# Two small matrix products per unit spread over all four 64x64 quadrants of TensorE, in a kernel that runs a linear-attention recurrence and a mixture of experts

## The chip, the cores and the metric

The kernel runs on one core of one Trainium2 chip. The metric is the device time of one execution in microseconds (us); lower is better. Before the change it was 1084.33 us, the median of 3 runs (1083.53 to 1084.63). The engines are called PE (TensorE matmul), PEld (TensorE's weight loads), ACT (ScalarE), DVE (VectorE), POOL (GpSimd) and SP (SyncE, which issues most transfers here).

## The reference

Two blocks follow each other. The first is a recurrence over 768 tokens, for 4 batches and 8 heads, with a 40x40 state per head; the second a mixture of 4 experts on the 3072 rows of 320 numbers that the first leaves.

```python
for t in range(S):
    y[:, :, t] = np.einsum('bhd,bhde->bhe', rt, state)
    Sa = np.einsum('bhde,bhe->bhd', state, at)
    state_decay = state * wt[:, :, None, :] - np.einsum('bhd,bhe->bhde', Sa, bt)
    state = state_decay + np.einsum('bhd,bhe->bhde', vt, kt)
...
p = domain_probs / (domain_probs.sum(-1, keepdims=True) + 1e-09)
for e in range(E):
    h = np.maximum(x @ w1[e], 0.0)
    out += p[:, e:e + 1] * (h @ w2[e])
```

All numbers are float32.

## The kernel before, in words

**Units.** The recurrence is cut into 12 chunks of 64 tokens. A unit is one chunk of two of the four batches: two batches x 64 tokens fill the 128 partitions, and the 8 heads lie beside each other. There are 24 units, numbered 0 to 23; units 0 and 1 are chunk 0, and so on. Within a chunk the recurrence becomes products of 64x64 matrices, among them the inverse of a triangular 64x64 matrix per batch and head.

**Stages of a unit.** `within` (L451) prepares a unit: decays (G, gp), the scaled inputs N, K and AT, their transposed copies NT and KT (ACT), and the score matrices. The scores pc are masked into VC by DVE (`causal`, L449, two copies, one per bank), pe into ET in the same way, and pfe becomes F (ACT, L580), the matrix to be inverted. `substitute` (L627) inverts the four 32x32 diagonal blocks of it: ACT and DVE copy them out (blocks, L632), DVE forms M, and POOL (DVE in unit 0) substitutes forward over 32 columns (tile Z, L670 and L687). `merge` (L693) makes the 64x64 inverse out of the 32x32 ones. `step` (L731) then runs the unit's step of the recurrence: prn (products with the state), psat, pxr, pdy, and the result Y, which goes to the mixture as xT. The mixture's products (ph, p, po) are cut into pieces and put between the recurrence's products, so that PE has dense work while others prepare the next small product.

**The order on the engines.** PE's instructions run in the order in which the code makes them (`stated`, `in_order`; `matmul` is the helper at L110, so every product has that line). DVE's order is written out in `VECTOR_ORDER` for a large part of the work. ACT's order is set by a scheduler from priorities (`sooner` raises one). In the main loop the order on PE around the change is, for units 6 to 22: the transposes pNT and pKT, the product pc of a later unit, then pY of `merge`, then prn of `step` (two products, with AT and with the identity), a first part of ph, pQ of `merge`, the rest of ph and a product p of the mixture.

**Quadrants.** Small products use 64 rows (contraction) by 64 columns (output partitions) of the 128x128 array: a quadrant is a row half and a column half. `quadrants` (L432) issues the heads of a product in the order of `QUADS`, which visits all four quadrants, and gives each row half its own PSUM bank (`banks`, two of them). `two_heads` inside `merge` (L709) is different: row half r always goes to column half r, into one bank.

**PSUM.** The eight banks are dealt from two pools: `big`, five banks, for the recurrence, and `mm`, three banks, for the mixture. A tile that asks for a bank of `big` gets one that an earlier tile has left, and its first matmul waits until the copy out of that earlier tile is done. The five banks go round among pg, pNT, pKT, pc (2), pY (1), prn (2), pQ (1), pfe (2), psat (2), pe (2), pxr (2), pev (2) and pdy (2).

**The merge.** Z's result is transposed into Qc and QTc (DVE). First product: pY, of below and QTc (below is the off-diagonal 32x32 block of F, copied by POOL), copied by ACT to Yq with four copies of 32 partitions x 128 elements. Second: pQ, of Qc and Yq, copied with four more into the off-diagonal block of QT (the diagonal blocks of QT are POOL's copies, L705). psat and the product after it read QT.

Of the kernel before, what the change touches and what calls it, by code (L numbers as in the profile page):

```python
# [33 lines left out]
def kernel(  # L34
# [38 lines left out]
    nc = tc.nc  # L73

    B, H, S, D = r.shape
# [3 lines left out]
    Q = 32  # L79
# [10 lines left out]
    def noted(ins, name, n=None, i=None):  # L90
        if n is None:
            n = sum(k.startswith(name) for k in made)
        key = f"{name}{n}" if i is None else f"{name}{n}.{i}"
        made[key] = ins
        if key in names:
            stated_order.append(ins)
        return ins

    def keep(ins):

        if not any(ins is x for x in stated_order):
            tc.keep_in_program_order(ins)
# [6 lines left out]
    def matmul(**k):  # L109
        return stated(nc.tensor.matmul(**k))  # L110
# [11 lines left out]
    def of_mixture(name):  # L122
# [6 lines left out]
        out=ident[:], in_=ident[:], pattern=[[1, P]], compare_op=ALU.is_equal, fill=0.0,  # L129
# [5 lines left out]
    for t, n, op in ((upf, L, ALU.is_gt), (diagf, Q, ALU.is_equal)):  # L135
        nc.vector.memset(t[:], 1.0)
        for q in range(P // n):
            o = slice(q * n, (q + 1) * n)
            nc.gpsimd.affine_select(
                out=t[o], in_=t[o], pattern=[[1, n]], compare_op=op, fill=0.0, base=0, channel_multiplier=-1,  # L140
# [3 lines left out]
    def dealt(x):  # L144

        return x.rearrange("p h (k g) -> p k g h", g=4)
# [54 lines left out]
    for n, a_sum in enumerate(("a1", "a7", "a5", "a2")):  # L201
        t = padded["RV"[n % 2], n // 2] = sb.tile([P, H, 64], FP32, name="padded", tag=a_sum)
# [21 lines left out]
    def sooner(wanted):  # L224
        return tc.high_priority(offset=SOONER) if wanted else nullcontext()
# [68 lines left out]
    ins = nc.vector.transpose(out=unit_cols[:], in_=dealt(diagf[:, None, :].to_broadcast([P, H, Q])))  # L294
# [88 lines left out]
    def half(s):  # L383
        return slice(64 * s, 64 * s + 64)

    def quarter(q):
        return slice(Q * q, Q * q + Q)

    def of_slot(x, s):

        return x.rearrange("p (j s) e -> p j s e", s=2)[:, :, s, :]
# [301 lines left out]
    def merge(q):  # L693


        Qc = sb.tile([P, H, Q], FP32, name="Qc", tag="q", bufs=2)
        QTc = sb.tile([P, H, Q], FP32, name="QTc", tag="q", bufs=2)
        keep(noted(nc.vector.transpose(out=dealt(Qc[:]), in_=q.Z), "Qc", q.u))
        ins = nc.vector.transpose(  # L699
            out=QTc[:].rearrange("p h r -> p (h r)"), in_=Qc[:].rearrange("p h c -> p (h c)"),  # L700
        )
        keep(noted(ins, "QTc", q.u))
        q.QT = QTs()
        for i in range(P // Q):
            ins = nc.gpsimd.tensor_copy(out=q.QT[quarter(i), :, quarter(i % 2)], in_=QTc[quarter(i)])  # L705
            tc.keep_in_program_order(ins)
        yield

        def two_heads(name, lhsT, rhs, to):  # L709
            p = (of_mixture if q.u == 0 and name == "pY" else big)(name)  # L710
            for n in range(NJ):
                for r in range(2):
                    matmul(
                        out=p[half(r), n * 2 * Q:(n + 1) * 2 * Q], lhsT=lhsT[half(r), 2 * n:2 * n + 2, :],
                        rhs=rhs[half(r), 2 * n:2 * n + 2, :], start=True, stop=True,
                    )
            for r in range(2):
                for y in range(2):
                    src = p[quarter(2 * r + y), 0:H * Q].rearrange("p (n two t) -> p n two t", two=2, t=Q)[:, :, y, :]
                    with sooner(name == "pY"):  # L720
                        ins = nc.scalar.copy(out=of_slot(to[quarter(2 * r)], y), in_=src)
                    noted(ins, name + "c", q.u, 2 * r + y)

        Y = Ys()
        two_heads("pY", q.below, QTc, Y)
        yield

        two_heads("pQ", Qc, Y, q.QT[:, :, quarter(1)])
        yield

# [476 lines left out]
    for u in range(1, NU):  # L1207
        in_order[0] = True
        q = units[u]
# [149 lines left out]
```

## Time and profile before

| | |
|---|---|
| median of 3 runs | 1084.33 us |
| span of the profiled execution, first to last instruction | 1081.0 us |
| what the runs have beyond that span | 3.3 us |
| mean granted TensorE clock | 0.995 |
| PE busy, 0 to 54 us | 44.80 of 54.00 us |
| PE busy, 54 to 234 us | 178.02 of 180.00 us |
| PE busy, 277 to 948 us | 671.00 of 671.00 us |
| ACT busy, 277 to 948 us | 227.90 us |
| DVE busy, 277 to 948 us | 488.22 us |
| matmul records of pY, of pQ | 384 and 384, 16 a unit |
| ACT copies Yq<-pY, QT<-pQ | 96 and 96, 4 a unit, 0.256 us each |

The profile is one execution; its time is given as the span, and the run's time has some us around it. Times within it are counted from the start of the span. A matmul of 32-bit numbers shows as two records of the profile, and a weight load as two as well. The view called timeline merges neighbouring instructions of one kind: start, length, engine, line, operation, output<-input, tile and shape, count, and in brackets how long the engine was idle before and what released it.

### The profile page before, as it was taken

The page shows a single profiled execution, that of the slowest core. Times are in us where ns is not written, and L with a number is a line of the kernel's source. Part 1 is how long each engine was busy: PE and PEld are TensorE (multiplying, and loading weights), DVE is VectorE, ACT ScalarE, POOL GpSimd, SP SyncE. Part 2 cuts the span into 40 slices and gives each one's busy share as a digit, 9 for nine tenths or more (in the row PEclk, how much of TensorE's full clock was granted, in tenths as well). Part 3 has the DMA queues.
Part 4 walks back from the last instruction along what each step waited for, and adds up shares of the span by engine and source line. Part 5 has one row for each costly group of instructions (what it writes and reads, how often), then busy time and mean ns, then how long its engine had stood idle before and what let it go on. Part 6 is the DMA issues. An engine that isn't in the chain of part 4 may idle for free.

```text
span 1081.0 us, 38617 instructions
## 1 busy us (share of the span) xinstructions
PE 1066.3 (99%) x16140; PEld 960.2 (89%) x16140; DVE 760.2 (70%) x1549; ACT 353.3 (33%) x958; POOL 494.2 (46%) x1276
## 2 busy tenths in 40 slices
PE   7899999999999999999999999999999999999998
PEld 7788888899999999999999999999989999998888
DVE  7687779897776866877777768668767776534343
ACT  3442435333333424224333334242333333221110
POOL 5116777765264373473562643734725626420000
PEclk9899999999999999999999999999999999999999
DMA  7877645435436445444364363454443532322320
GB/s 117 228 188 211 145 107 125 89 103 142 100 87 155 110 104 127 114 108 112 91 138 100 97 148 96 102 124 109 115 94 107 133 88 62 98 76 78 104 78 13
DMA packets 268870, 122.20 MB, mean 113 GB/s; under 512 B 213736, under 2 KB 242072, under 8 KB 268696
## 3 DMA queue, kind: packets, MB, share of 16 engines
q1 hardware_dynamic: 264712, 118.90, 45.1%
q8 instruction: 127, 2.08, 0.8%
q10 hardware_dynamic: 3984, 0.84, 0.4%
q14 instruction: 47, 0.39, 0.1%
HBM read 111.79 MB, written 3.93 MB: 107 GB/s over the span
## 4 chain that ended last, share of the span: by engine, by line
PE 86%; POOL 8%; DVE 3%; issue 2%; ACT 1%; DMA 0%; ACTq 0%; DVEq 0%; POOLq 0%
PE ph L110 36%; PE p L110 30%; POOL Z L687 5%; POOL Z L670 3%; PE pdy L110 3%; PE psat L110 2%; PE pxr L110 2%; PE prn L110 2%; PE po L110 2%; PE pc L110 1%; PE pfe L110 1%; PE pev L110 1%; PE pe L110 1%; PE warm L110 1%; PE pQ L110 1%
## 5 line engine op out<-in xcount | busy, mean ns | idle before, releaser
L110 PE MATMUL ph<-xT,w1p 128*128 128x256 f32 (+3 forms) x3040 | 441.6, 375 | 0.1
L110 PEld LDWEIGHTS ph<-xT,w1p 64*64 64x64 f32 (+1 forms) x3040 | 336.9, 161 | 53.8 <-issue 13.0
L687 POOL TENSOR_TENSOR Z<-Z 128x31 f32<-128x31 f32 (+7 forms) x704 | 261.3, 371 | 55.2
L1000 DVE TENSOR_TENSOR a<-hs 128x512 f32<-128x512 f32 x220 | 152.5, 711 | 107.8 <-ACT hs L877 107.8
L877 ACT ACTIVATE hs<-ph 128x512 f32<-128x512 f32 (+1 forms) x208 | 116.8, 564 | 322.6 <-PE ph L110 322.2
L670 POOL TENSOR_TENSOR Z<-M,Z 128x62 f32<-128x62 f32 (+7 forms) x352 | 145.7, 414 | 95.0 <-DVE M L656 69.2
L110 PE MATMUL p<-sums,a 128*128 128x160 f32 x1056 | 164.9, 299 | 0.0
L110 PEld LDWEIGHTS p<-sums,a 128*128 128x128 f32 x1056 | 152.8, 190 | 2.2
L892 DVE SCALAR_TENSOR_TENSOR osb<-p,gate,osb 128x320 f32<-128x320 f32 (+1 forms) x243 | 108.0, 481 | 65.6 <-PE p L110 60.3
L637 POOL COPY below<-F 32x256 f32<-32x256 f32 x48 | 21.3, 443 | 232.8 <-ACT F L580 231.1
L110 PEld LDWEIGHTS p<-w,hs 128*128 128x128 f32 x704 | 98.6, 190 | 8.5 <-issue 7.3
L110 PE MATMUL p<-w,hs 128*128 128x160 f32 x704 | 104.9, 302 | 0.0
L110 PE MATMUL p<-w,a 128*128 128x160 f32 x704 | 102.8, 299 | 0.0
L110 PEld LDWEIGHTS p<-w,a 128*128 128x128 f32 x704 | 98.0, 190 | 0.0
L705 POOL COPY QT<-QTc 32x256 f32<-32x256 f32 x96 | 40.3, 420 | 72.7 <-DVE QTc L699 67.2
L797 ACT COPY RS<-pxr 64x256 f32<-64x256 f32 x88 | 32.2, 366 | 102.7 <-DVE SX L449 79.6
L618 ACT COPY EV<-pev 64x160 f32<-64x160 f32 x96 | 23.0, 286 | 90.5 <-PE pev L110 90.1
L518 DVE RECIPROCAL gp<-gp 128x320 f32<-128x320 f32 x24 | 51.6, 2151 | 0.7
L640 DVE STREAM_TRANSPOSE M<-blocks 128x1024 f32<-128x1024 f32 x24 | 47.2, 1967 | 2.6 <-ACT blocks L632 2.5
L449 DVE COPY_PREDICATED VC<-mask_up,pc 128x256 f32<-128x256 int32 x48 | 18.7, 443 | 40.8 <-PE pc L110 40.8
L580 ACT COPY F<-pfe 128x256 f32<-128x256 f32 x48 | 15.6, 376 | 79.6 <-PE pfe L110 78.7
L110 PE MATMUL pdy<-VC,k_tok 64*64 64x104 f32 (+1 forms) x768 | 38.4, 259 | 2.6 <-issue 2.6
(151 smaller groups left out, 1346.7 us busy)
## 6 DMA issues: line engine op xcount, KB each, us to landing
w1p<-in_moe_w_dram SPq DMA_DIRECT2D x95, 512.0 KB
w1p<-in_moe_w_dram SPq DMA_DIRECT2D x190, 64.0 KB
w<-in_moe_w_dram SPq DMA_DIRECT2D x4, 1280.0 KB
sums<-in_moe_w_dram SPq DMA_DIRECT2D x9, 512.0 KB
natW<-in_w_dram SPq DMA_DIRECT2D x48, 80.0 KB
natB<-in_b_dram SPq DMA_DIRECT2D x48, 80.0 KB
natK<-in_k_dram SPq DMA_DIRECT2D x48, 80.0 KB
out_dram<-osb SPq DMA_DIRECT2D x45, 80.0 KB
```

Source lines behind the costliest of these rows:

```text
L110: return stated(nc.tensor.matmul(**k))
L518: pin(noted(nc.vector.reciprocal(out=gp[:], in_=gp[:]), "1/gp", q.u))
L618: nc.scalar.copy(out=of_slot(q.EV[half(p)], i ^ p)[:, :, 0:D], in_=pev[i][half(p)])
L637: tc.keep_in_program_order(nc.gpsimd.tensor_copy(out=q.below[quarter(i)], in_=q.F[quarter(i), :, 0:Q]))
L640: ins = nc.vector.transpose(out=M[:], in_=cols)
L670: ins = eng.tensor_tensor(out=Z[:, 1:3, 0:n, j + 1:Q], in0=M[:, j:j + 2, None, j + 1:Q].to_broadcast([P, 2, n, m]), in1=Z[:, here, 0:n, j: ...
L687: eng.tensor_tensor(out=z[:, 0], in0=z[:, 0], in1=z[:, x], op=ALU.add)
L705: ins = nc.gpsimd.tensor_copy(out=q.QT[quarter(i), :, quarter(i % 2)], in_=QTc[quarter(i)])
L797: nc.scalar.copy(out=RS[half(s), x ^ s::2], in_=prs[x][half(s)].rearrange("p (j i) t -> p j i t", i=2),)
L877: ins = nc.scalar.activation(out=h[:, i * HF // 2:(i + 1) * HF // 2, 0:n], in_=ph[i][:], func=ACTF.Relu,)
L892: ins = nc.vector.scalar_tensor_tensor(out=to, in0=p, scalar=sc, in1=to, op0=ALU.mult, op1=ALU.add)
L1000: ins = nc.vector.tensor_tensor(out=t[:], in0=x, in1=y, op=op)
```

## The change

`two_heads` takes two banks, one for each row half r of the operands. The n-th pair of heads writes the column half r for even n and the other one for odd n, so that the eight matmuls of a product visit the quadrants (0,0), (1,1), (0,1), (1,0) twice. The results of even and odd pairs now lie in different partition halves of a bank, so each copy out of PSUM is split in two by `odd`: eight copies of 32 partitions x 64 elements in place of four of 32 x 128. Both products of all 24 units are made so; in unit 0 the two banks of pY are from the pool `mm`.

```diff
         def two_heads(name, lhsT, rhs, to):
-            p = (of_mixture if q.u == 0 and name == "pY" else big)(name)
+            p = [(of_mixture if q.u == 0 and name == "pY" else big)(name) for _ in range(2)]
             for n in range(NJ):
                 for r in range(2):
                     matmul(
-                        out=p[half(r), n * 2 * Q:(n + 1) * 2 * Q], lhsT=lhsT[half(r), 2 * n:2 * n + 2, :],
+                        out=p[r][half(r ^ n % 2), n * 2 * Q:(n + 1) * 2 * Q], lhsT=lhsT[half(r), 2 * n:2 * n + 2, :],
                         rhs=rhs[half(r), 2 * n:2 * n + 2, :], start=True, stop=True,
                     )
             for r in range(2):
-                for y in range(2):
-                    src = p[quarter(2 * r + y), 0:H * Q].rearrange("p (n two t) -> p n two t", two=2, t=Q)[:, :, y, :]
-                    with sooner(name == "pY"):
-                        ins = nc.scalar.copy(out=of_slot(to[quarter(2 * r)], y), in_=src)
-                    noted(ins, name + "c", q.u, 2 * r + y)
+                for odd in range(2):
+                    for y in range(2):
+                        src = p[r][quarter(2 * (r ^ odd) + y), 0:H * Q]
+                        src = src.rearrange("p (n two t) -> p n two t", two=2, t=Q)[:, odd::2, y, :]
+                        with sooner(name == "pY"):
+                            ins = nc.scalar.copy(out=of_slot(to[quarter(2 * r)], y)[:, odd::2, :], in_=src)
+                        noted(ins, name + "c", q.u, 4 * r + 2 * odd + y)
```

## The prediction

> **What bounds the kernel now.** I read the page first, its busy rows and the slices.
>
> ```profile
> span 1081.0 us, 38617 instructions
> PE 1066.3 (99%) x16140; PEld 960.2 (89%) x16140; DVE 760.2 (70%) x1549; ACT 353.3 (33%) x958; POOL 494.2 (46%) x1276
> PEclk9899999999999999999999999999999999999999
> ```
>
> TensorE is busy for 1066.3 of 1081.0 us at a granted clock of 0.995. Cut into stretches, 277 to 948 us has PE busy for 671.00 of 671.00 us, so there every nanosecond added to or taken from PE's queue arrives at the end. Before 234 us the chain of waits runs for long pieces through POOL Z (the inverse of units 3 to 6); there PE idles about 1 us between 108 and 234 us, so two chains run nearly level.
>
> Next the timeline of one steady unit, PE alone. A matmul of this kernel is two records, so a two_heads product (8 matmuls) is 16, a four-quadrant product (16 matmuls) is 32.
>
> ```profile
> 574.24 0.69 PE L110 MATMUL pc<-RT,VT 40*64 40x64 f32 x32
> 574.75 0.57 PE L110 MATMUL pY<-QTc,below 64*64 64x64 f32 x13
> 575.18 0.59 PE L110 MATMUL prn<-state,AT 64*64 64x40 f32 x28
> 576.15 0.39 PE L110 MATMUL ph<-xT,w1p 64*64 64x256 f32 x2
> ...
> 577.02 0.63 PE L110 MATMUL pQ<-Yq,Qc 64*64 64x64 f32 x16
> 577.58 0.48 PE L110 MATMUL ph<-xT,w1p 128*128 128x256 f32 x1
> ...
> 595.56 0.65 PE L110 MATMUL pxr<-RT,SaT 64*64 64x64 f32 x32
> 596.03 0.65 PE L110 MATMUL pxr<-RT,SN 64*64 64x64 f32 x32
> ```
>
> The reader is to see the pace. pxr, which uses all four quadrants in the order the change gives to pY and pQ, moves 32 records in 596.03 - 595.56 = 0.47 us, 0.0147 us each. In the records pQ starts a pair (one per diagonal quadrant) every 0.058 us: 16 records take 8 x 0.058 = 0.47 us, half the work in the same time. Then the same unit on ACT and DVE.
>
> ```profile
> 574.43 0.60 ACT L524 COPY KT<-pKT 128x512 f32<-128x512 f32 x1
> 575.43 1.07 ACT L721 COPY Yq<-pY 32x128 f32<-32x128 f32 x4 [0.40 <-PE pY L110]
> 577.70 1.06 ACT L721 COPY QT<-pQ 32x128 f32<-32x128 f32 x4 [0.18 <-PE pQ L110]
> ...
> 575.00 0.79 DVE L449 COPY_PREDICATED VC<-mask_up,pc 128x256 f32<-128x256 int32 x2 [2.26 <-PE pc L110]
> ```
>
> The first VC copy empties pc's second bank; it takes 0.444 us (median of its 48), so it ends at 575.44. Today nobody near waits for it: prn has begun at 575.11.
>
> **The change part by part.** *PE, removed:* each product goes from 0.47 to 16 x 0.0147 = 0.235 us, a gain of 0.23 us. The trace has it for pxr, pe and prn, so I take it as it is; 48 products would give 11.3 us if nothing waited.
>
> The Trainium skill, TensorEngine Tiling (Array Packing), section Theoretical Speedup, promises up to 2x for each dimension of 64 or less, which agrees with the half; taken alone it would make the sum 1081.0 - 11.3 = 1069.7 us (an estimate). Its section Gotcha 1: PSUM Pressure warns that row tiles need banks of their own, and that is what decides here.
>
> *Banks, added wait:* pY and pQ now take two of the five "big" banks each. In the built instruction order every queue keeps its order apart from a few QT copies on ACT, but the waits move: in units 6 to 22 the first matmul into prn's second bank, which waited for ACT's copy KT, now waits for DVE's copy VC out of pc's second bank. PE is in order, so all of prn, the ph behind it and pQ stand behind that matmul. In the steady units 7 to 22: VC ends 575.44; the hand-over to PE costs between 0.05 us (ACT's Yq to pQ in unit 4) and 0.15 us (SX to pdy in unit 0, 38.37 to 38.51, through an extra semaphore instruction). The new wait is a single one, so I take 0.08, plus 0.05 us of slow first step, seen when pQ restarts in unit 4. So prn's stream begins at 575.57 instead of 575.22 (its 64 records at 0.0147 end at 576.15, where ph takes over): +0.35. The 0.23 us that pY saves is swallowed by this wait, because VC starts when pc is done, whatever pY does. pQ's 0.23 is kept. Net +0.12, with bounds 0 (575.44 taken without any hand-over: +0.22 - 0.23) and +0.25. Times 16: **+2.0** (0 to +4.0).
>
> *Unit 6:* there DVE does two sums of weights first, and VC starts at 235.78, 1.25 us after pY (234.53). Its end at 236.22 plus 0.13 is 236.35 against 235.00: +1.35, less pQ's 0.23: **+1.1** (0.9 to 1.3).
>
> *Copies, added:* eight of 64 elements replace four of 128. No row has 64. ACT copies of 64x160 take 0.287 and of 64x256 0.366 us, 0.82 ns an element; 32x128 takes 0.256, so 64 elements cost 0.256 - 64 x 0.00082 = 0.20 us, bounded by 0.13 (half) and 0.256 (no gain). Four start 0.27 apart today, so eight at 0.22 last 7 x 0.22 + 0.20 = 1.74 us against 1.07: +0.67.
>
> The Trainium skill, ScalarE: Activation LUTs, section What ACT_TABLE_LOAD costs, gives 186 ns plus 0.833 ns an element, with 93 ns of overlap; that would be 293 ns for 128 elements, where this trace has 256, and starts 0.20 apart, where it has 0.27. By the page eight copies last about 1.26 us, which would shrink the early term below from 1.4 to about 0.3 and the sum to 3.2; the trace decides.
>
> In a steady unit nothing feels it: Yq starts about 575.20 (pY is done earlier, KT ends 575.03) and ends about 576.95, while PE, late by 0.35, reaches pQ at 577.37. Without that stall PE would come at 576.79 and wait some 0.2 us: the stall hides the copies. SN and the eight QT copies end near 579.5; the next hs is ready at 579.67, and psat, which reads QT, runs at 586.96.
>
> *Early units, where PE waits for Yq already:*
>
> ```profile
> 170.06 1.07 ACT L721 COPY Yq<-pY 32x128 f32<-32x128 f32 x4
> 170.78 0.91 PE L110 MATMUL pQ<-Yq,Qc 64*64 64x64 f32 x12
> 171.19 0.43 PEld L110 LDWEIGHTS pQ<-Yq,Qc 64*64 64x64 f32 x12 [0.27 <-ACT Yq L721]
> ```
>
> Here the second half of pQ starts when the last Yq copy lands. Where ACT is free, the copies start 0.23 earlier, end 0.67 - 0.23 later, and pQ's rest is 0.23 shorter: +0.2 in units 1 and 3. In units 2, 4 and 5 ACT is busy (SN; hs) and the start does not move: +0.67 - 0.23 = +0.44 each. PE together 1.7. POOL's chain: in unit 2 F and blocks stand behind Yq on ACT, and one QT copy now stands ahead of blocks: 0.67 + 0.22, with unit 1's 0.2 it is 1.1. At 234.04 PE waited 0.27 us for DVE's RT, behind POOL; so PE leads there, with 1.7 - 0.27 = **+1.4** (0.5 to 2.6). Unit 0 loses up to 0.9 through both copies; I cost it at nothing, because at 40.16 to 42.49 PE stands 2.3 us for "issue", which names no releaser; if that cover moves along, it is the 0.9 in the upper bound. prn in units 3 to 5 now waits for a DVE copy ET, inside the time that pQ waits for Yq: nothing.
>
> *Unit 23:* no VC wait; 0.47 gained, some 0.25 lost to Yq: **-0.2**.
>
> **Sum:** 2.0 + 1.1 + 1.4 - 0.2 = +4.3 us on the profiled 1081.0, so a span of 1085.3. The median of the runs, 1084.33, is 3.3 above the span; I add the same 4.3: **1088.6 us**. Bounds: 0 + 0.9 + 0.5 - 0.4 = +1.0, and 4.0 + 1.3 + 2.6 - 0 = +7.9.
>
> **Rivals.** *No change:* hand-over near nothing and the early delays partly hidden, +1 to +2, 1085.3 to 1086.3. For it: pQ's gain and the stall are within 0.1 us of each other. Against: 0.05 us is the shortest hand-over I found. 0.11.
>
> *Faster:* the VC copy does not hold prn. Then units 6 to 22 gain two products each less the 0.2 us wait for Yq, 17 x (0.47 - 0.2) = 4.6, less 1.4 early, plus unit 23's 0.2: -3.4, 1080.9 us. It decides once VC ends before about 575.25 in that unit, 0.2 us earlier than it does; DVE idles 2.26 us ahead of VC waiting for pc, so it can't begin earlier. 0.07.
>
> *The four quadrants do not run together* with two products of one row half in one bank: no gain in pQ, so 16 x 0.35 + 1.35 + 1.4 + 5 x 0.23 = +9.5, 1093.8 us. Against: pxr writes its banks in the same way at 0.0147 us a record. 0.05.
>
> *Forecast*, slower by +2.2 to +8: 0.77.
>
> **How the numbers follow.** What this kernel's measurement can tell from no change is about 0.2%, 2.2 us. Slower holds the forecast and the quadrant rival, 0.82; same 0.11; faster 0.07. The range runs from 1085.0, which takes in most of the no-change case, to 1092.3, the upper bound of the sum.
>
> **What would show it.** pQ from its first record to the ph behind it should fall from 0.56 to 0.33 us. In the waits a new row of PE's weight loads or matmuls prn behind DVE VC should stand with some 17 entries, near 0.3 us each and 1.3 the longest. Yq copies should last 0.20 us. VC to VC of neighbouring units should be 0.1 us further apart. I am wrong if prn begins before VC's first copy ends, if that gap shrinks, or if PE's idle time before 234 us has not grown.

## The result and the profile after

| | before | after |
|---|---|---|
| median of 12 runs each, on the same chips | 1082.36 us (1079.31 to 1084.63) | 1086.39 us (1083.86 to 1089.85) |
| ratio, 95% interval | | 1.0036 (1.0024 to 1.0048) |
| span of the profiled execution | 1081.0 us | 1088.1 us; a second one 1082.7 us |

The kernel became slower by 0.36%, some 3.9 us; 4.3 us had been forecast. In absolute time 1086.39 us stands against 1088.6, because the forecast was built on the first three runs of before, whose median of 1084.33 us lies 2.0 us above that of the twelve. The granted clock does not differ: its mean over the twelve runs of the changed kernel is 0.996, as it is over the 17 and the 27 runs of the kernel before that stand beside the experiments. The profiled execution of the changed kernel happened to be the longest of its twelve, so spans of single profiles are not subtracted from each other below; distances within a unit are, and a second profile of the same kernel stands beside the first.

The page of the changed kernel, its span, busy row, clock row and the group of the new copies:

```profile
span 1088.1 us, 38848 instructions
PE 1066.2 (98%) x16140; PEld 958.8 (88%) x16140; DVE 761.5 (70%) x1549; ACT 381.0 (35%) x1150; POOL 493.6 (45%) x1276
...
PEclk9899999999999999999999999999999999999999
...
L723 ACT COPY Yq<-pY 32x64 f32<-32x64 f32 x192 | 38.9, 203 | 12.3 <-PE pY L110 9.7
```

PE issues the same 16140 records and is busy as long as before (1066.3 us), at the same clock, so the added time is time in which it stands. ACT is busy 27.7 us longer: 192 more copies. One of 64 elements takes 203 ns; 0.20 us had been estimated. Cut into the same stretch as before:

```profile
277.00:948.00 671.00, 669.24 (x10486) 612.11 (x10485) 486.56 (x981) 246.93 (x742) 325.74 (x861) 1.00 0.46 108
```

The columns after the length are busy us of PE, PEld, DVE, ACT and POOL, then granted clock, DMA share and GB/s. PE, which had been busy for all of these 671.00 us, now stands for 1.76 of them. The timeline of unit 14, the unit shown of before:

```profile
579.86 0.69 PE L110 MATMUL pc<-RT,VT 40*64 40x64 f32 x32
580.37 0.41 PE L110 MATMUL pY<-QTc,below 64*64 64x64 f32 x16
580.71 1.02 PE L110 MATMUL prn<-state,AT 64*64 64x40 f32 x29
582.10 1.04 PE L110 MATMUL ph<-xT,w1p 64*64 64x256 f32 x15
582.87 0.50 PE L110 MATMUL pQ<-Yq,Qc 64*64 64x64 f32 x16
583.30 1.56 PE L110 MATMUL ph<-xT,w1p 128*128 128x256 f32 x6
...
580.84 1.73 ACT L723 COPY Yq<-pY 32x64 f32<-32x64 f32 x8 [0.18 <-PE pY L110]
...
580.62 0.77 DVE L449 COPY_PREDICATED VC<-mask_up,pc 128x256 f32<-128x256 int32 x2 [2.17 <-PE pc L110]
```

pY is through in 0.41 us where it took 0.57 and more, and then prn's first group takes 1.02 us in place of 0.59. Inside that row, record by record, prn starts two records (580.71 and 580.78) and none until 581.12. VC's first copy, begun at 580.62, ends at 581.06; the rest of prn runs 0.06 us later. That is the new wait. The eight Yq copies end at 582.57, before PE asks for them at 582.87. The waits of the changed kernel (us in total, times, longest):

```profile
PEld prn L110 <- DVE VC L449: 4.7, 17, 1.1
PE pdy L110 <- issue: 4.0, 2, 3.4
PEld pQ L110 <- ACT Yq L723: 3.0, 8, 0.6
```

The first row is new, with one entry for each of the units 6 to 22: 1.1 us in unit 6 and (4.7 - 1.1) / 16 = 0.23 us in the others. The third stood at 1.2 us and 4 entries before: the early units. The second is a stall of unit 0 that the last section comes back to.

### The profile page after: what moved, and what is told of

The parts are those of the page before. It is cut to its first block, busy times and chain, and to the rows that moved or that the text cites. A ratio compares the mean times of both kernels' runs of the same rounds, so it can differ in the third digit from the quotient of the medians.

```text
span 1088.1 us, 38848 instructions
## 1 busy us (share of the span) xinstructions
PE 1066.2 (98%) x16140; PEld 958.8 (88%) x16140; DVE 761.5 (70%) x1549; ACT 381.0 (35%) x1150; POOL 493.6 (45%) x1276
## 3 DMA queue, kind: packets, MB, share of 16 engines
q8 instruction: 127, 2.08, 0.8%
## 4 chain that ended last, share of the span: by engine, by line
PE 86%; DVE 6%; POOL 4%; issue 2%; ACT 1%; DMA 1%; DVEq 0%; POOLq 0%; ACTq 0%
PE ph L110 37%; PE p L110 29%; PE pdy L110 3%; POOL Z L687 2%; PE po L110 2%; PE prn L110 2%; PE psat L110 2%; PE pxr L110 2%; POOL Z L670 1%; PE pfe L110 1%; PE pc L110 1%; PE pev L110 1%; PE pe L110 1%; PE pNT L113 1%; PE pg L113 1%
## 5 line engine op out<-in xcount | busy, mean ns | idle before, releaser
L687 POOL TENSOR_TENSOR Z<-Z 128x31 f32<-128x31 f32 (+7 forms) x704 | 255.1, 362 | 55.2
L670 POOL TENSOR_TENSOR Z<-M,Z 128x62 f32<-128x62 f32 (+7 forms) x352 | 151.1, 429 | 95.2 <-DVE M L656 69.3
L723 ACT COPY Yq<-pY 32x64 f32<-32x64 f32 x192 | 38.9, 203 | 12.3 <-PE pY L110 9.7
```

The lines of the kernel that those rows point to most:

```text
L670: ins = eng.tensor_tensor(out=Z[:, 1:3, 0:n, j + 1:Q], in0=M[:, j:j + 2, None, j + 1:Q].to_broadcast([P, 2, n, m]), in1=Z[:, here, 0:n, j: ...
L687: eng.tensor_tensor(out=z[:, 0], in0=z[:, 0], in1=z[:, x], op=ALU.add)
L723: ins = nc.scalar.copy(out=of_slot(to[quarter(2 * r)], y)[:, odd::2, :], in_=src)
```

## The experiments

The table sets all kernels side by side. The columns in the middle are for unit 14, in us from pY's first record: last record of prn, end of the Yq copies, first record of pQ, first record of the ph behind it. The last three are the change, against the profile of before, in the distance between pY of the named units; they come from one profile each and scatter by up to 1 us, as the two rows of after show.

| kernel | ratio (95% interval) | prn last | Yq end | pQ | ph | units 1-6 | 6-7 | 7-23 |
|---|---|---|---|---|---|---|---|---|
| before | 1 | 1.35 | 1.75 | 2.27 | 2.83 | | | |
| after | 1.0036 (1.0024 to 1.0048) | 1.69 | 2.19 | 2.50 | 2.93 | +2.1 | +1.0 | +2.5 |
| after, second profile | one run | 1.69 | 2.20 | 2.50 | 2.93 | +1.1 | +0.9 | +1.3 |
| e1 copies | 1.0051 (1.0033 to 1.0069) | 1.35 | 2.41 | 2.26 | 2.95 | +2.4 | +0.3 | +2.3 |
| e2 banks | 1.0059 (1.0041 to 1.0076) | 1.68 | 1.73 | 2.50 | 3.16 | +0.3 | +1.3 | +5.3 |
| e3 pQ alone | 0.9974 (0.9962 to 0.9987) | 1.35 | 1.75 | 2.20 | 2.59 | +0.9 | -0.3 | -2.4 |
| e4 pY alone | 1.0080 (1.0061 to 1.0098) | 1.68 | 2.19 | 2.50 | 3.16 | +2.4 | +0.9 | +4.9 |
| e5 other bank for pY | 0.9980 (0.9967 to 0.9993) | 1.27 | 2.20 | 2.08 | 2.62 | +1.3 | -0.1 | -3.4 |
| e6 e5, pY late | 0.9973 (0.9959 to 0.9987) | 1.27 | 2.20 | 2.08 | 2.62 | +0.5 | -0.1 | -2.5 |
| e7 pQ alone, late | 0.9960 (0.9947 to 0.9974) | 1.35 | 1.75 | 2.20 | 2.59 | +0.1 | -0.2 | -3.1 |

Each ratio is against runs of the kernel before on the same chips. The theory is that of the prediction: the banks delay prn by VC's copy, which swallows pY's gain; pQ's gain is kept; the copies cost only where PE already waits for them. Its rivals: the copies are the loss, or the four quadrants bring nothing.

### e1_copies: the eight copies alone

```diff
-                for y in range(2):
-                    src = p[quarter(2 * r + y), 0:H * Q].rearrange("p (n two t) -> p n two t", two=2, t=Q)[:, :, y, :]
+                for odd in range(2):
+                    for y in range(2):
+                        src = p[quarter(2 * r + y), 0:H * Q].rearrange("p (n two t) -> p n two t", two=2, t=Q)[:, odd::2, y, :]
...
```

> The kernel before, with each copy out of pY and pQ split in two (eight of 64 elements), one bank and the diagonal quadrants as before. Bank theory (the loss comes from prn behind VC): no row prn behind DVE VC; but with no stall to hide them the eight Yq copies end near 2.45 us after pY's start, where pQ comes at 2.27, so a steady unit loses about 0.2 us at pQ, the early units 0.6 each: +5 to +7 us, 1.005 to 1.006. Copies theory (the copies alone make the loss, in ACT's time): the loss of the change, about +4, in the same places as there, prn included. If the copies were free: 0.

Measured: 1.0051. The timeline of its unit 14:

```profile
578.72 0.76 PE L110 MATMUL pQ<-Yq,Qc 64*64 64x64 f32 x16
579.41 0.92 PE L110 MATMUL ph<-xT,w1p 128*128 128x256 f32 x3
...
577.14 1.73 ACT L722 COPY Yq<-pY 32x64 f32<-32x64 f32 x8 [0.40 <-PE pY L110]
```

Yq ends at 578.87, and pQ, begun at 578.72, has to wait within itself: 0.69 us to the ph behind it, 0.13 more than before. No matmul of prn waits for VC. So the copies by themselves cost 0.13 us in each steady unit and some 2.4 us in the early ones. In the changed kernel the steady 0.13 is not paid, because there PE comes 0.3 us after the last copy. That the stall hides the copies is thereby shown. In the sum the copies alone lose as much as the whole change (1.0051 against 1.0036), so the time alone could not have told the theories apart; the places do.

### e2_banks: the second bank alone, diagonal quadrants, four copies

```diff
-            p = (of_mixture if q.u == 0 and name == "pY" else big)(name)
+            p = [(of_mixture if q.u == 0 and name == "pY" else big)(name) for _ in range(2)]
...
-                        out=p[half(r), n * 2 * Q:(n + 1) * 2 * Q], lhsT=lhsT[half(r), 2 * n:2 * n + 2, :],
+                        out=p[r][half(r), n * 2 * Q:(n + 1) * 2 * Q], lhsT=lhsT[half(r), 2 * n:2 * n + 2, :],
...
```

> The kernel before, with a bank for each row half in both products, but the diagonal quadrants and the four copies as before: the banks alone. Bank theory: 17 entries of prn behind DVE VC, prn's last record 0.33 us later after pY's start in units 7 to 22 (1.35 to 1.68) and 1.3 in unit 6, nothing given back: 16 x 0.33 + 1.3 = +6.6 us, 1.006. Copies theory: no loss, 1.000. Quadrant theory (the spread product itself is slower): no loss, 1.000.

Measured: 1.0059. Its unit 14:

```profile
578.83 0.89 PE L110 MATMUL prn<-state,AT 64*64 64x40 f32 x29
...
580.86 0.73 PE L110 MATMUL pQ<-Yq,Qc 64*64 64x64 f32 x16
581.53 0.70 PE L110 MATMUL ph<-xT,w1p 128*128 128x256 f32 x2
```

prn's last record is at 1.68, as in the changed kernel, though pY here takes as long as before: what times prn is VC. The second bank brings pY itself nothing: it takes 0.41 us from its first to its last record with two banks and with one. The ph behind pQ is 0.33 us late in each steady unit, and 16 x 0.33 = 5.3 is what units 7 to 23 show. In its waits only unit 6 stands as a row of prn behind VC (1.1 us): in the others prn's first records run into the tail of pY's, and the engine counts as busy. A wait that such a list does not show can still be the one that costs.

The Trainium skill, TensorEngine Tiling (Array Packing), section Gotcha 1: PSUM Pressure, warns of the extra banks without a price; here it is 0.33 us a unit and 1.3 us in unit 6.

### e3_pq_only: pQ alone spread

```diff
-            p = (of_mixture if q.u == 0 and name == "pY" else big)(name)
+            apart = name == "pQ"
+            pool = of_mixture if q.u == 0 and name == "pY" else big
+            p = [pool(name) for _ in range(2 if apart else 1)]
+            p = p if apart else p * 2
...
```

With `apart` the quadrants and the copies are those of the change, without it those of the kernel before.

> Two banks, four quadrants and eight copies in pQ alone; pY as before the change. Bank theory: prn waits for ACT's KT as before the change, nothing behind VC; pQ to the ph behind it falls from 0.56 to about 0.33 us in 23 units, 23 x 0.23 = -5.3 us, 0.995. Copies theory: the eight QT copies cost about half of the change's loss: +2, 1.002. Quadrant theory: 0 or a loss.

Measured: 0.9974, some 2.8 us faster than before where 5.3 was expected. In the steady units it does what it should: prn is as before, and the ph behind pQ stands at 2.59 in place of 2.83. So the four quadrants do run together, and two banks for pQ cost nothing there.

The gain that the expectation had counted for units 1 to 6, some 1.2 us, did not come: they show +0.9. POOL's chain gained nothing from a faster pQ. From Qc of unit 1 to Qc of unit 6 it takes 0.5 us more than before, here and in e6, which spreads the early pQ as well, and 0.1 us more in e7, which does not. PE cannot get ahead of that chain: at unit 6 of the kernel before it waits 0.3 us for RT, which DVE transposes right after Qc. In this one profile PE came later still. It stands for 1.0 us in pxr between units 5 and 6, a wait with the releaser "issue", and pY of unit 6 begins 0.4 us further behind Qc than before. Nothing in the trace ties that stall to the change.

### e4_py_only: pY alone spread

The same edit with `apart = name == "pY"`.

> Two banks, four quadrants and eight copies in pY alone; pQ as before the change. Bank theory: prn 0.33 later in units 7 to 22 and 1.3 in unit 6, early units 0.4 to 0.7 each for the copies, nothing won at pQ: 6.6 + 2.5 = +9 us, 1.008. Copies theory: half of the change's loss, +2, 1.002.

Measured: 1.0080. In its waits:

```profile
PEld prn L110 <- DVE VC L449: 4.3, 17, 0.8
```

The wait is that of the changed kernel, and pY's own gain is nowhere to be seen: ph stands at 3.16 as in e2, where pY was not faster. The difference to the changed kernel, 1.0080 against 1.0036 or some 4.8 us, has the size of pQ's gain: ph comes 0.23 us earlier there (2.93) in each steady unit.

### e5_py_mm: the change, with pY's second bank from the mixture's pool

```diff
-            p = [(of_mixture if q.u == 0 and name == "pY" else big)(name) for _ in range(2)]
+            p = [(of_mixture if name == "pY" and (q.u == 0 or r == 1 and q.u > EARLY) else big)(name) for r in range(2)]
```

(Against the changed kernel; from unit 6 on.) The banks of `big` go round as before up to prn, so the wait for VC is gone without any wait being taken out.

> The changed kernel, but from unit 6 on pY's second bank comes from the pool of the mixture (three banks), so prn gets back the banks it had and waits for ACT's KT. Bank theory: no prn behind DVE VC from unit 6 on; pY's gain is then cut to some 0.13 us by KT (ends 0.28 after pY's start) and pQ comes early, so that its second half waits for the eighth Yq copy (2.19 after pY's start): the ph behind pQ starts near 2.6 after pY's start where the kernel before has 2.83. 17 x -0.2 = -3.4 with +1.4 of early units: -2 us, 0.998. If the lost time were in the copies or the quadrants: it stays at the change's +4, 1.004.

Measured: 0.9980, faster than before. Its unit 14:

```profile
574.37 0.71 PE L110 MATMUL prn<-state,AT 64*64 64x40 f32 x29
...
576.22 0.61 PE L110 MATMUL pQ<-Yq,Qc 64*64 64x64 f32 x16
576.76 1.35 PE L110 MATMUL ph<-xT,w1p 128*128 128x256 f32 x5
...
574.60 1.74 ACT L723 COPY Yq<-pY 32x64 f32<-32x64 f32 x8 [0.18 <-PE pY L110]
```

prn starts 0.23 us after pY and runs through. The turn from +0.36% to -0.20%, with all else of the change in place, shows that the bank rotation made the loss from unit 6 on; units 1 to 6, whose banks are those of the change, still lose 1.3 us to the copies. What is late next also shows: PE reaches pQ at 576.22, the last Yq copy lands at 576.34, and pQ takes 0.54 us to the ph behind it, where e3 has 0.39. Of pY's gain of 0.23 us, that leaves nothing: ph at 2.62 stands against 2.59 in e3, where pY is not spread.

### e6_py_mm_late: as e5, with pY spread from unit 6 on alone

```diff
+            apart = name == "pQ" or q.u > EARLY
+            p = [pool(name)]
+            if apart:
+                p.append((big if name == "pQ" else of_mixture)(name))
+            p = p if apart else p * 2
...
```

`EARLY` is 5.

> pQ spread in all units (as in the run with pQ alone), and pY spread from unit 6 on with its second bank from the mixture's pool. Bank theory: each steady unit's ph behind pQ starts 2.55 to 2.6 after pY's start, as with pQ alone (2.59), because KT and the Yq copies take what pY gives: -3 to -5 us, 0.995 to 0.998, not clearly better than pQ alone. If the copies had a cover here: another 17 x 0.23 = -4, 0.993.

Measured: 0.9973. Within the intervals it is no better than e3: spreading pY in the steady units gains nothing even with the right bank, since its copies hold pQ.

### e7_pq_late: pQ alone, from unit 6 on

```diff
+            apart = name == "pQ" and q.u > EARLY
...
```

The other lines are those of e3.

> pQ spread from unit 6 on only. If the gain of the early units is lost behind POOL's chain, which leads up to unit 6: 18 x -0.23 = -4 us, 0.996, the same as pQ in all units within the noise. If the early units' gain counts: 1.3 us worse than pQ in all units, 0.9985.

Measured: 0.9960, the fastest of all, 1078.32 us against 1082.54 for the kernel before beside it. Its unit 14:

```profile
577.04 0.46 PE L110 MATMUL pQ<-Yq,Qc 64*64 64x64 f32 x16
577.43 1.35 PE L110 MATMUL ph<-xT,w1p 128*128 128x256 f32 x5
```

The distances of units 1 to 6 are those of before, and each unit from 6 on is some 0.2 us shorter. Whether it beats e3 is not settled by the times, since the intervals overlap; for it speaks POOL's chain, as e3 shows.

### after_again: a second profile of the changed kernel

> The changed kernel once more, for a second profile. Steady units as in the first: prn's last record 1.68 after pY's start, pQ at 2.50. The first profile was of the slowest of 12 runs; if its extra 3 us lie ahead of unit 3 (PE's wait for issue in pdy, 3.4 us there), this one's pY of unit 3 stands 1 to 2 us earlier than the first's and the span is near 1084.

Measured: 1084.43 us, span 1082.7. The rows that answer to the first profile (PE itself has no row for pdy behind "issue" here; PEld had 5.1 us in 5 entries in the first profile):

```profile
PEld prn L110 <- DVE VC L449: 4.6, 17, 1.0
...
PEld pdy L110 <- issue: 0.9, 4, 0.3
```

The wait for VC is the same, and so is every distance in unit 14. The difference lies ahead of it: pY of unit 1 is 3.2 us earlier than in the first profile, and of unit 3 3.8 us; 1 to 2 had been expected. From unit 1 to unit 23 the first profile loses 5.5 us on the profile of before, the second 3.3, so the 3.9 of the medians lies between. The 1.0 us between the two in units 1 to 6 stands in pdy of unit 1 (0.57 us) and pxr of unit 5 (0.46 us).

## Why the prediction was right

**What bounds the kernel** was read rightly: PE is full, so 0.23 us taken out of its queue in each steady unit arrives at the end (e7), and so does 0.33 us put in (e2).

**PE's gain.** A product was to gain 0.23 us. From the last quadrant record of ph to the ph behind pQ it is 0.77 us before, 0.54 after and 0.53 in e3: 0.23 to 0.24. The sign that the prediction named, pQ's first record to ph falling to 0.33, came out at 0.43: its first record also stands 0.11 us behind ph and no longer 0.21, in e2 as well, where pQ gains nothing. The mark was ill chosen, the gain was not.

The Trainium skill, TensorEngine Tiling (Array Packing), section Theoretical Speedup, promises up to a factor of two; the 0.24 us out of 0.47 here agree with it.

**The wait for VC** came where it was foretold, in units 6 to 22 with 17 entries. The hand-over from VC to prn takes 0.06 us, inside the 0.05 to 0.15 that the prediction had; prn moved by 0.33 us against 0.35, and the net in a steady unit is +0.10 against +0.12. Units 7 to 23 show +2.5 and +1.3 us in the two profiles, against 2.0; the first has a jump of 0.5 between units 17 and 18 that the second lacks. It arises in a ph some 12 us behind pY, which the change does not touch, at a granted clock of 1.00; e3 has such jumps at the same place of units 13 and 19, and what makes them is not known. The entries of the wait came out at 0.23 us where near 0.3 had been named, and the longest at 1.1 where 1.3 had been; prn's first two records run before the wait. One of the signs against the forecast, prn beginning before VC's first copy ends, was thus met by the letter, though the product does not go on until VC is done.

**Unit 6:** +1.0 and +0.9 against 1.1.

**The copies:** 1.73 us against 1.74, at 0.203 us each, 0.22 apart. e1 bears out both halves of the argument, the cost in the early units and the cover in the steady ones. Without that cover the price is 0.13 us; the prediction had some 0.2, reckoned with PE earlier than it is in e1. In e5, where PE is that early, pQ takes 0.15 us longer than in e3.

The Trainium skill, ScalarE: Activation LUTs, section What ACT_TABLE_LOAD costs, states 186 ns plus 0.833 ns an element and an overlap of 93 ns; an estimate by it is 239 ns for 64 elements. The trace has 203 ns and starts 219 ns apart, so the measurement decides, and eight copies last longer than by the page.

**The early units:** units 1 to 6 lost 2.1 and 1.1 us, against 1.4. Unit by unit, the end of pQ after pY moved by +0.21, +0.42, +0.21, +0.28 and +0.29 us in units 1 to 5, where 0.2, 0.44, 0.2, 0.44 and 0.44 had been worked out; the price was too high in units 4 and 5.

**Unit 0** was costed at nothing. Its products do come later: from pY to the product of SX in pdy it is 6.53 us in the profile of before and 7.27 and 7.92 in the two of after. In the second profile the stall behind fell to 0.1 us, and the next product, pNT, begins at 43.07 us, against 43.01 before. That is not the cover alone, because the granted clock was low there, 0.72 from 32 to 44 us, against 0.98 in the profile of before and 0.89 in the first of after. The plainer case is e1, which has the eight copies in unit 0 too: at a granted clock of 1.00 its pNT begins at 42.68 us. In the first profile of after the stall ran to 43.82 us and pNT stood at 44.73. So the cover worked in two of these three, and a long stall by itself is no work of the change: in e7, where unit 0 is as before, it lasts 3.3 us too. What releases PE there stays open.

**Unit 23:** +0.3 and +0.1 from 22 to 23, and -0.2 in both from there to the end, against -0.2; too small to settle.

**The rivals.** That VC does not hold prn is refuted by e2 and e4; e5 is close to that rival as it would have been, and its price of -3.4 us lies inside e5's interval, -0.8 to -3.6 us about the -2.2 measured; it had 0.27 us for a steady unit, where e5 gains 0.20. That the copies make the loss is refuted for the steady units by e2, which loses there without them, and by e5, which gains there with them; in units 1 to 6 they are the loss, as forecast (+2.4 us in e1, +0.3 in e2). That the quadrants do not run together is refuted by e3. No change is excluded by the interval, whose lower end, 1.0024, stands just above 0.2%.

**Luck.** The mechanism came out as named, and each term of the sum lies within 1 us of what the profiles show. That the sum lies within 0.4 us of the measured 3.9 is in part luck: two profiles of the same kernel differ by 1.0 us in units 1 to 6 and by 1.1 us in units 7 to 23.

## What to carry to other kernels

A product that takes one bank more moves every later tile of its pool on to another bank: look up whose copy frees that bank, and whether an in-order engine stands behind it, before counting what the product saves. Judge each product of a paired change by itself; here one gained, and the other gained nothing even when its bank was right, since its smaller copies came late. A gain on a full engine counts in full (pQ from unit 6 on, 0.23 us a unit), and one ahead of a chain that another engine leads does not (pQ in units 1 to 5, behind POOL).

## What was not expected of the hardware

- PE stops in the middle of pdy in unit 0 and waits for nothing that the profile shows. In ten profiles the gap from record to record is 0.1 to 3.7 us; eight times it ends between 42.16 and 42.93 us, wherever it began (39.14 to 41.48). One kernel's two profiles differ by 3.2 us ahead of unit 1, nearly the size of the effect under study, while unit 14 agrees to 0.01 us. Of the 3.2 us, 1.7 lie ahead of pNT (44.73 and 43.07 us), and 1.6 between it and pY of unit 1.
- That second part goes with the granted clock. In the 6 us from pNT on it is 0.70 in the first profile of after, 0.72 in that of before, 0.97 in the second of after and 1.00 in e1, and from pNT to pY of unit 1 it is 25.49, 25.43, 23.94 and 23.87 us. From 50 us on it is 1.00 in all four, which the mean of 0.995 over the span does not show.
- ACT's copies of half the size take 0.203 us against 0.256: half the elements save a fifth of the time.
- A product that is held by a bank does not show this at its first record: two records of prn run, and the 0.34 us hole stands within the product, where a list by groups shows a longer row and the list of waits, in e2, nothing.
